# One transpose instruction for a whole cache tile, in a fused decode attention and gated MLP with gradients

## The chip, the cores and the metric

The kernel runs on one core of a Trainium2 chip. The metric is the time of the program on the device in microseconds; three runs of the kernel before gave a median of 469.5 us (469.31 to 469.81). One more execution was taken by the hardware profiler; its page and its trace are what is read here. Engines go by the profile's names: PE (TensorE), DVE (VectorE), ACT (ScalarE), POOL (GpSimd) and SP, which here only issues transfers.

## What is computed

The reference computes an output and all gradients (a vjp with a given `grad_out`) of one decode step:

```python
xn = layernorm(x)                                  # x: 2 x 1 x 576, bf16
q = (xn @ wq), 32 heads of 128                     # each pair of heads shares one of 16 cache heads
p = softmax(q . k_cache * 128**-0.5)               # caches: 2 x 16 x 4096 x 128
out = x + (p . v_cache) @ wo + ((xn @ w_gate) * (xn @ w_up)) @ w_down      # MLP width 4608
# returned: out and the gradients of x, k_cache, v_cache, wq, wo, w_gate, w_up, w_down
```

There is one query position, so the arithmetic is small beside the data: both caches and all weights are read once, and gradients of the same sizes are written. The gradient of each cache head is an outer product of 4096 values with the query or with the incoming gradient.

## The kernel before, in words

**Tiles.** A cache head of one batch row is 4096 x 128 bf16, 1 MB. It is loaded by one transfer into a tile of 128 partitions x 4096 elements (`kv_t`), 32 positions in each partition. Sixteen such buffers (`big`) are shared by cache tiles (at most 6), transposed tiles `X` (at most 10), store tiles `st` (at most 5) and MLP weights; they are handed out as they come free. A step `s` (16 in all) treats two cache heads of one batch row: two tiles of K and two of V, 64 cache tiles in all. Two steps make a group, which also has a slice of `wq` and of `wo`; the MLP goes in nine slices beside the groups.

**A cache tile's way.** `load_kv` (L1133) loads it from SP's queue. `turn` (L1208) takes an `X` buffer and transposes the tile into it on DVE. The transpose (`t32`, L464, recorded as L465) works on 32 x 32 blocks, and the bf16 data is seen as fp32 words, so that two neighbouring bf16 elements, a pair, move together: 4096 elements are 2048 pairs in each partition. `turn` does this in two halves of 1024 pairs, and sets the event `xE` after the second. Only then do the scores start: `score` (L1261, matmuls of L1267) reads columns from all over `X`, for K in `softmax` (L1317), for V in `dscore` (L1373). The untransposed tile is read once more by `contract` (L1424, matmuls of L1441), which sums over positions. When that and the transposes are done, `free_kv` (L1419) gives the cache buffer back, and the next load may be issued.

**The softmax chain.** It is a ping-pong of short instructions. DVE takes the maximum of each partition (`ex`, `mx`, L1330), PE turns it, DVE reduces it (`m`, L1340), ACT spreads it (`mr`, L1342), PE multiplies (L1344), DVE makes the bias (`negb`, L1346), ACT takes the exponential (L1349), PE sums (L1352), DVE inverts (`rz`, L1354), ACT scales, PE spreads, ACT or DVE copies (`sp`), and DVE transposes the result (`pp`). `dscore` is alike for the gradient of the scores: DVE multiplies and sums (`ds`, `cs`, L1385), PE sums over partitions (L1391), DVE makes `cr` (L1393) and `ds` (L1396), PE spreads it, ACT or DVE copies it (`sp`), DVE transposes it (`dd`). From `pp` and `dd` the outer products (L1289) make the gradients of the caches: `unit` (L698) has PE fill two PSUM banks, and ACT (L469) or DVE (L471) copy 1024 columns of them to a store tile; `put` (L691, transfer at L695) stores it. Smaller DVE copies serve a group's projections: `qd` (L992), `rep` (L1006), `oT` (L1461), `rT`.

**What sets the order.** The kernel does not leave the order to a scheduler of the compiler. Every piece of work is a Python generator that asks the planner `Order` (L105) for an engine and a time before it records its instructions: `yield DVE(1.25)` asks for 1.25 us of DVE, and the instructions that follow in the generator are recorded when the planner grants it. Requests have priorities (`pr`); buffers and events are planned as well. So each engine has a fixed order in which its instructions run, one behind the other, and what an engine waits for holds all that is behind it. `turn` asks twice for each tile, and between the two grants the planner may put other work on DVE.

Of the kernel before, what the change touches and what calls it, by code (L numbers as in the profile page):

```python
# [250 lines left out]
def DVE(cost):  # L251
    return ("op", "DVE", cost)
# [14 lines left out]
def ACQ(tag):  # L267
    return ("acq", tag)
# [6 lines left out]
def WAIT(*events):  # L275
    return ("wait", events)


def SET(event):
    return ("set", event)  # L280
# [6 lines left out]
def PRIO(prio):  # L287
    return ("prio", prio)
# [59 lines left out]
def pr(name, s):  # L348
    edge = {} if type(s) is not int else HEAD if s < 2 else TAIL if s > 13 else {}
    return STEP * s + PR[name] + edge.get(name, 0) + OFF.get(name, {}).get(int(s), 0)  # L350
# [3 lines left out]
def kernel(  # L354
# [106 lines left out]
    def pairs(ap):  # L461
        return ap.bitcast(FP32)

    def t32(out, in_):  # L464
        nc.vector.transpose(out, in_)  # L465
# [742 lines left out]
    def turn():  # L1208
        for s in range(NS):
            for t in range(2):  # L1210
                yield PRIO(pr(f"turn{t}", s))
                for l in range(G):
                    yield WAIT(kvL[s][t][l], *([] if s + t == 0 else [grp[s // Bq]["Ed" if t else "Eq"]]))
                    x = yield ACQ("X")
                    src = kv_t[kvS[s][t][l]]
                    for h in range(2):
                        yield DVE(1.25)
                        t32(pairs(X_t[x][:, 2048 * h:2048 * h + 2048]), pairs(src[:, 2048 * h:2048 * h + 2048]))
                    xS[s][t][l] = x
                    yield SET(xE[s][t][l])  # L1220

# [335 lines left out]
    for gen in (turn(), fronts(), build_W(0), build_W(1), build_BD(), attend(), dscores(), backs()):  # L1557
        od.spawn(gen, 0.0)
# [33 lines left out]
```

## Time and profile before

| | |
|---|---|
| median of three runs | 469.5 us |
| profiled execution, its own time | 469.68 us |
| its span, from the first to the last instruction | 467.9 us |
| DVE: busy, instructions | 373.8 us, 711 |
| transposes of a `big` tile from a `big` tile (L465, 1024 pairs) | 146, 176.3 us in all, 1224 ns each |
| evictions on DVE (L471) and on ACT (L469) | 81.3 us (75), 272.5 us (303) |
| moved by DMA | 185.97 MB, 397 GB/s on average |
| load of a K tile, a V tile, from issue to landing (median) | 14.5 us, 13.5 us |

Of the 146 transposes 128 are the halves of cache tiles; 18 serve the MLP weights (L938 and below) and are not touched. A line of a timeline or of a list of groups gives the start and the length in us (or busy us and the mean in ns), the engine, the line of the code, and what was written and read; the bracket at its end tells how long the engine had been idle before, and what released it. The chain that ended last is followed back from the last instruction, at each step to what released it. A slice of the page's rows is a fortieth of the span, 11.7 us.

### The profile page before, as it was taken

How to read it: one execution, taken by the hardware profiler on the slowest of the kernel's cores; microseconds unless marked ns; L12 is line 12 of the kernel's file. 1: busy time of each engine (PE TensorE's matmuls, PEld its weight loads, DVE VectorE, ACT ScalarE, POOL GpSimd, SP SyncE). 2: the span in 40 equal slices, each digit the busy share in tenths (PEclk: the TensorE clock that was granted, in tenths of full speed). 3: DMA queues.
4: the chain of work that ended last, by engine and by line, in shares of the span. 5: the costliest groups of instructions: out<-in, count | busy, mean ns of one | idle time of the engine just before them, and what ended most of it. 6: DMA issues, size and time to landing. Idle time of an engine off the chain costs nothing.

```text
span 467.9 us, 15712 instructions
## 1 busy us (share of the span) xinstructions
PE 378.5 (81%) x6750; PEld 216.3 (46%) x6750; DVE 373.8 (80%) x711; ACT 334.6 (72%) x512; POOL 143.6 (31%) x174
## 2 busy tenths in 40 slices
PE   1688779697987888797888887789988988988886
PEld 1445455465443444454555354455524433544443
DVE  8887888797589897769987779788878866877883
ACT  3268648788786787665867775678778968787874
POOL 0740044303316443470016341500643316033200
PEclk9966775987566666756775676755666665666865
DMA  8999999999999999999999999999999999999995
GB/s 300 417 407 423 409 423 396 415 411 330 418 423 406 410 424 410 421 416 421 404 398 416 414 415 405 378 345 366 419 415 424 420 414 426 422 351 393 420 367 207
DMA packets 40710, 185.97 MB, mean 397 GB/s; under 512 B 3640, under 2 KB 12352, under 8 KB 24256
## 3 DMA queue, kind: packets, MB, share of 16 engines
q1 hardware_dynamic: 40636, 184.96, 98.5%
q8 instruction: 53, 0.87, 0.7%
q14 instruction: 17, 0.14, 0.1%
q10 hardware_dynamic: 4, 0.00, 0.0%
HBM read 92.48 MB, written 92.48 MB: 395 GB/s over the span
## 4 chain that ended last, share of the span: by engine, by line
DMA 45%; PE 24%; DVE 13%; ACT 9%; SPq 4%; issue 4%; POOL 1%; DVEq 0%; ACTq 0%; POOLq 0%
DMA big<-in_A_v_cache_dram 22%; DMA out_dram<-big 15%; ACT big L469 7%; DVE big L465 7%; DMA ww<-in_B_w_down_dram 4%; PE ps_o L1289 4%; DMA big<-in_B_w_up_dram 4%; PE ps_m L1441 3%; PE ps_m L1267 3%; DVE big L471 3%; PE ps_o L726 3%; PE ps_o L763 2%; SPq L1191 2%; SPq L1197 1%; PE ps_m L677 1%
## 5 line engine op out<-in xcount | busy, mean ns | idle before, releaser
L469 ACT CAST big<-ps_o 128x1024 bf16<-128x1024 f32 (+2 forms) x303 | 272.5, 956 | 51.4 <-PE ps_o L1289 29.5
L465 DVE STREAM_TRANSPOSE big<-big 128x1024 f32<-128x1024 f32 x146 | 176.3, 1224 | 18.9 <-DMA big<-in_A_v_cache_dram 5.3
L1255 POOL TENSOR_TENSOR BD<-vr,mask 128x2048 bf16<-128x2048 bf16 x32 | 115.3, 3605 | 121.1 <-PE ps_o L1289 43.0
L471 DVE CAST big<-ps_o 128x1024 bf16<-128x1024 f32 (+1 forms) x75 | 81.3, 1087 | 15.3 <-PE ps_o L1289 5.7
L1267 PE MATMUL ps_m<-big,W 128*32 128x128 bf16 x2048 | 61.1, 284 | 3.0 <-issue 1.7
L1232 POOL COPY W<-rep 32x16 bf16<-32x16 bf16 x128 | 24.9, 194 | 116.5 <-DVE rep L1006 95.5
L1267 PEld LDWEIGHTS <-W 128*32 128x32 bf16 x2048 | 48.0, 127 | 22.0 <-issue 21.1
L1289 PE MATMUL ps_o<-BD,pp 32*128 32x512 bf16 x256 | 45.6, 492 | 13.1 <-ACT big L469 8.0
L1289 PE MATMUL ps_o<-BD,dd 32*128 32x512 bf16 x256 | 45.5, 525 | 9.2 <-ACT big L469 6.8
L465 DVE STREAM_TRANSPOSE big<-ww 128x1152 f32<-128x1152 f32 (+1 forms) x25 | 33.0, 1321 | 4.5 <-DMA out_dram<-big 2.4
L1441 PE MATMUL ps_m<-big,pp 128*32 128x512 bf16 x256 | 31.5, 576 | 3.4 <-DVE pp L465 3.1
L1441 PE MATMUL ps_m<-big,dd 128*32 128x512 bf16 x256 | 29.7, 556 | 1.2 <-DVE dd L465 0.9
L1289 PEld LDWEIGHTS <-pp 32*128 32x128 bf16 x256 | 10.2, 97 | 32.9 <-issue 24.5
L1289 PEld LDWEIGHTS <-dd 32*128 32x128 bf16 x256 | 10.2, 99 | 24.7 <-issue 17.1
L1038 POOL COPY qr<-qd 128x256 bf16<-128x256 bf16 x8 | 3.2, 397 | 54.0 <-DVE qd L471 43.2
L763 PEld LDWEIGHTS <-xnr 32*128 32x128 bf16 x368 | 13.0, 122 | 13.0 <-issue 12.2
L726 PE MATMUL ps_o<-dyr,R 32*32 32x288 bf16 x256 | 17.3, 388 | 1.6 <-ACT big L469 1.5
L726 PE MATMUL ps_o<-dyr,hb 32*32 32x288 bf16 x288 | 15.9, 334 | 2.4 <-ACT big L469 2.2
L763 PE MATMUL ps_o<-D,xnr 32*128 32x128 bf16 x256 | 14.6, 293 | 3.9 <-issue 2.2
L1451 ACT ACTIVATE osb<-ps_m 128x512 bf16<-128x512 f32 x15 | 8.9, 596 | 8.6 <-PE ps_m L1441 8.3
L887 PE MATMUL ps_m<-big,Wdy 128*128 128x128 bf16 x162 | 14.8, 262 | 0.0
L677 PE MATMUL ps_m<-big,wm 128*32 128x128 bf16 x416 | 13.3, 287 | 1.3 <-DVE qd L992 0.6
(205 smaller groups left out, 489.6 us busy)
## 6 DMA issues: line engine op xcount, KB each, us to landing
out_dram<-big SPq DMA_DIRECT2D x74, 1024.0 KB, 13.6
big<-in_A_k_cache_dram SPq DMA_DIRECT2D x32, 1024.0 KB, 14.5
big<-in_A_v_cache_dram SPq DMA_DIRECT2D x32, 1024.0 KB, 13.5
out_dram<-big SPq DMA_DIRECT2D x17, 576.0 KB, 10.7
ww<-in_B_w_down_dram SPq DMA_DIRECT2D x9, 576.0 KB, 12.6
ww<-in_A_wo_dram SPq DMA_DIRECT2D x8, 576.0 KB, 8.4
ww<-in_A_wq_dram SPq DMA_DIRECT2D x8, 512.0 KB, 11.6
big<-in_B_w_gate_dram SPq DMA_DIRECT2D x4, 1024.0 KB, 14.5
```

What stands on the lines that cost most here:

```text
L465: nc.vector.transpose(out, in_)
L469: nc.scalar.copy(out, in_)
L471: nc.vector.tensor_copy(out=out, in_=in_)
L677: nc.tensor.matmul(dp[32 * q:32 * q + 32, 0:P], lhsT=W, rhs=view(X, 0, P, xoff(q, s), [[FS, 4], [2, 32]]), start=(s == 0), stop=(s == S - 1))
L726: nc.tensor.matmul(o[32 * q:32 * q + 32, aa, 0:HD2], lhsT=view(t, 32 * q, 32, 2 * A + aa, [[4, 32]]), rhs=dyr[32 * q:32 * q + 32, k * HD2: ...
L763: nc.tensor.matmul(o[:, aa, j * P:(j + 1) * P], lhsT=xnr[32 * a:32 * a + 32, dc * P:(dc + 1) * P], rhs=rhs(a), start=True, stop=True)
L887: nc.tensor.matmul(dh, lhsT=Wdy[:, e, 2 * k:2 * k + P], rhs=view(X[:], 0, P, 64 * k + e, [[D, FC], [2, 32]]), start=(k == 0 and e == 0), s ...
L1232: nc.gpsimd.tensor_copy(view(W_t[t][w][:], 32 * a, 32, 6 + 8 * a, [[G * WW, 4], [WW, G], [1, 2]]), view(rep_t[grp[g]["qs"]][:], 32 * a, 32 ...
L1255: nc.gpsimd.tensor_tensor(BD_t[i][:], view(vr_t[v][:], 0, P, 0, [[0, 16], [1, Dh]]), view(mask16[:], 0, P, 0, [[1, 16], [0, Dh]]), ALU.mult)
L1267: nc.tensor.matmul(sc[32 * cq:32 * cq + 32, :], lhsT=view(W[:], 0, P, (be * G + l) * WW + 6 - 4 * c2 - 2 * l, [[1, 32]]), rhs=view(X[:], 0 ...
L1289: nc.tensor.matmul(o[:, k, :], lhsT=pr2[32 * c4:32 * c4 + 32, :], rhs=BD[32 * c4:32 * c4 + 32, 8 * l + 4 * h2:8 * l + 4 * h2 + 4, :], star ...
L1441: nc.tensor.matmul(ct[32 * j:32 * j + 32, :], lhsT=view(rT, 0, P, 4 * c + 2 * l, [[1, 32]]), rhs=kv_t[kvS[s][t][l]][:, Dh * c:Dh * (c + 4) ...
```

## The change

`turn` records one transpose for the whole tile, 2048 pairs, where it recorded two for 1024 pairs each. Both requests to the planner stay, and stand on both sides of the one instruction, so the planner sees the same work and plans the same order as before. The one instruction is recorded at the place of the first half; what the planner put between the halves now stands behind the whole transpose. `xE` is set after the second request, as before.

```diff
                     src = kv_t[kvS[s][t][l]]
-                    for h in range(2):
-                        yield DVE(1.25)
-                        t32(pairs(X_t[x][:, 2048 * h:2048 * h + 2048]), pairs(src[:, 2048 * h:2048 * h + 2048]))
+                    yield DVE(1.25)
+                    t32(pairs(X_t[x][:]), pairs(src[:]))
+                    yield DVE(1.25)
                     xS[s][t][l] = x
                     yield SET(xE[s][t][l])
```

The orders of PE, ACT, POOL and SP are the same in both kernels. DVE has 64 instructions fewer. In 15 of the 64 tiles the halves stood directly one behind the other; in the other 49 one to six instructions stood between them.

## The prediction

> **What bounds the kernel now.** I read the page first: busy shares, DMA, chain.
>
> ```profile
> PE 378.5 (81%) x6750; PEld 216.3 (46%) x6750; DVE 373.8 (80%) x711; ACT 334.6 (72%) x512; POOL 143.6 (31%) x174
> ...
> GB/s 300 417 407 423 409 423 396 415 411 330 418 423 406 410 424 410 421 416 421 404 398 416 414 415 405 378 345 366 419 415 424 420 414 426 422 351 393 420 367 207
> ...
> DMA 45%; PE 24%; DVE 13%; ACT 9%; SPq 4%; issue 4%; POOL 1%; DVEq 0%; ACTq 0%; POOLq 0%
> ```
>
> DMA carries the span: most of the 40 slices move over 400 GB/s, and the chain that ended last is 45% transfers. But slices 10, 26 to 28 and 36 (330, 345 to 378, 351 GB/s) show that transfers were sometimes issued too late, and 46% of the chain is PE, DVE and ACT. There a late VectorE instruction lengthens the run. VectorE has 467.9 - 373.8 = 94.1 us free, so its busy time alone is not the limit; the moment at which each of its instructions ends is.
>
> **The price of the instruction.** The groups of VectorE by form give durations for three lengths:
>
> ```profile
> L465 DVE STREAM_TRANSPOSE big<-ww 128x1152 f32<-128x1152 f32 x17 | 23.2, 1365 | 3.2 <-DMA out_dram<-big 1.1 <-issue 1.1 <-DMA ww<-in_B_w_down_dram 0.9
> ...
> L465 DVE STREAM_TRANSPOSE big<-ww 128x1024 f32<-128x1024 f32 x8 | 9.8, 1227 | 1.3 <-DMA out_dram<-big 1.3
> ...
> L465 DVE STREAM_TRANSPOSE Xt<-big 128x512 f32<-128x512 f32 x6 | 4.0, 672 | 0.0
> ```
>
> From 1024 to 1152 pairs costs 138 ns, 1.08 ns a pair; from 512 to 1024 costs 555, also 1.08. So 2048 pairs should take 1225 + 1024 x 1.08 = 2.33 us. What two halves take today stands in VectorE's timeline:
>
> ```profile
> 349.75 2.35 DVE L465 STREAM_TRANSPOSE big<-big 128x1024 f32<-128x1024 f32 x2
> 352.02 0.14 DVE L1461 CAST oT<-ps_m 128x4 bf16<-128x4 f32 x1
> ```
>
> Two halves end after 2.35 us, not 2.45, because an instruction starts some 0.08 to 0.1 us before the one ahead of it ends; the next one starts after 2.27. The whole tile would let its successor start after 2.33 - 0.08 = 2.25. I take a saving of 0.02 us a tile, 64 x 0.02 = 1.3 us of VectorE. Bounds: at best all that is fixed in an instruction goes, 2 x 672 - 1227 = 0.12 us, 7.5 us in all; at worst the long instruction is slower than its two halves by the spread of the row (1190 to 1248 ns), 0.06 us, 3.7 us lost. [...]
>
> **What moves.** The diff keeps both requests to the planner, so PE, ACT, POOL and SP keep their order; only VectorE's changes. Where the planner put nothing between the halves (15 tiles) nothing else happens. In the other 49 tiles something stood between them, and now waits for the whole tile: it starts up to 1.1 us later (2.25 us after the tile's start instead of 1.15). The second half had covered the wait for the answer to it. The timeline of all engines shows one such place:
>
> ```profile
> 181.03 1.25 DVE L465 STREAM_TRANSPOSE big<-big 128x1024 f32<-128x1024 f32 x1
> ...
> 182.19 0.24 DVE L1340 TENSOR_REDUCE m<-ps_m 1x4 f32<-1x128 f32 x1
> 182.36 1.22 DVE L465 STREAM_TRANSPOSE big<-big 128x1024 f32<-128x1024 f32 x1
> 182.46 0.30 ACT L1342 COPY mr<-m 1x128 f32<-1x128 f32 x1 [0.37 <-DVE m L1340]
> ...
> 182.67 1.00 ACT L469 CAST big<-ps_o 128x1024 bf16<-128x1024 f32 x1
> ...
> 182.81 0.38 PE L1344 MATMUL ps_m<-one,mr 1*128 1x1 f32 x2
> ...
> 183.52 0.11 DVE L1346 TENSOR_SCALAR negb<-ps_m 128x1 f32<-128x1 f32 x1
> ```
>
> The maximum `m` is ready at 182.43; ACT spreads it, PE multiplies until 183.19, and `negb` follows: a round trip of some 0.8 us, all under the second half. After the change `m` starts at 181.03 + 2.25 = 183.28 and ends at 183.5, and `negb` starts at about 184.5: 1.0 us late, with VectorE idle meanwhile. Queued behind it on VectorE is an eviction (L471); on ACT the 1.00 us eviction behind `mr` waits just as long, and PE waits for the PSUM that they free, SP for the stores: its queue already waits 80.0 us for evictions of VectorE and 78.2 for those of ACT ahead of stores (L695).
>
> I went through the 49 tiles in the timeline in this way; times are starts of the first half:
> - `m` between, `negb` next (36.61, 181.03, 331.80, 354.58): 1.0 + 1.0 + 1.0 + 0.9 = 3.9 us.
> - `negb` between, `rz` next (19.81): 0.95.
> - `ex` and `mx` (L1330) between, `m` next (210.07, 399.53, 422.01): 0.3 + 0.4 + 0.5 = 1.2.
> - `cr` and `ds` between, `sp` or `dd` next (29.28, 151.74, 173.59, 369.30, 392.09): 0.5 + 0.45 + 0.7 + 0.45 + 0.45 = 2.55. From `ds` to `sp` the timeline shows 0.46 us (260.83 to 261.29).
> - a small copy whose answer from PE comes next (9.18 `xs`, 128.75 `oT`, 131.27 `rT`, 324.86 `qd`): 1.0 + 0.5 + 0.95 + 0.9 = 3.35.
>
> In sum 11.95 us of new waits. Elsewhere the tile now covers a wait that stood in front of the instruction between: 1.31 us (tile of 277.67), 0.73 (221.55), 0.56 (104.50), 0.49 (287.80), 0.38 (240.40), 0.34 (344.55) and six of 0.12 to 0.32, together 5.2 us. VectorE's own line is thus 11.95 - 5.2 - 1.3 = 5.4 us longer, beside 94 us of slack.
>
> **What reaches the end.** The chain in order of time has pieces of VectorE at these places:
>
> ```profile
> 181.03 1.25 DVE big L465
> 182.27 0.16 DVE m L1340
> 182.43 1.15 DVE big L465
> 183.58 0.04 DVE negb L1346
> ```
>
> Of the new waits, those at 36.61 (1.0), 173.59 (0.7), 181.03 (1.0), 210.07 (0.3), 354.58 (0.9) and 399.53 (0.4) lie on it, and those at 128.75 and 131.27 touch it through ACT and PE with about 0.2 each: 4.7 us. The others fall into its transfers (22 to 36, 146 to 157, 321 to 335, 381 to 399, 403 to 432 us), where the DMA queue hides them: a 1 MB transfer lands 13.5 to 14.5 us after its issue, while 1 MB at 420 GB/s is 2.5 us, so it mostly waits behind others. The covered waits lie beside the chain. For pairs on the chain the shorter instruction gives back about 0.2. Of the 4.5 us left I take a quarter off, because lateness ahead of a transfer that has to queue anyway is partly absorbed: 3.5 us. The profiled execution took 469.68 us (467.9 of span and 1.8 around it), 0.18 over the median of 469.5. So 469.5 + 3.5 = **473.0 us**.
> [...]
>
> **Rivals.**
> - *Faster: the tile is complete sooner.* The scores (L1267) wait for the whole tile, so splitting never helped them. Where much stood between, the tile ends far earlier: the tile of 277.67 takes 7.24 us from its start to its end and would take 2.3, 4.9 us less; that of 245.67 3.0 us less, those of 240.40 and 359.77 2.2 each. Then scores start and cache buffers come free sooner, and loads are issued sooner. Against it: in front of a cache load (L1142) SP's queue waits 16.9 us for stores, 8.7 for earlier loads and 7.4 for the contraction (L1441), and no transpose is among the longest. Price: the 5.2 us of covered waits and half of the 1.3 to 7.5 us of saving, at the chain's share of compute (about half): 3 to 4.5 us, so 465 to 466.5. It decides if the order of loads, not the softmax, sets the end. Chance 0.28.
> - *Hidden:* the DMA queue absorbs both; 469.5 within 1 us. For it: 94 us of slack. Against it: the slices of 330 to 378 GB/s, where it ran dry. Chance 0.12.
> - *The delay spreads:* ACT and PE take their instructions in order, so every new wait also holds evictions behind it, and all 12 us arrive: 481.5. Chance 0.12.
> - *The instruction gives no saving* (0.06 us slower a tile): 3.7 us of VectorE, less than half of it on the chain, within the forecast's own range.
>
> **How the numbers follow.** The forecast (470.4 to 478) has 0.48. The range 465.5 to 480.5 leaves out about 0.1 on each side. The repeated runs differ by 0.5 us, so 0.2% (0.94 us) is about the smallest change that a measurement can tell. Faster 0.28, same 0.12, slower 0.12 + 0.48 = 0.60.
>
> **What would show it.** Right: 64 instructions of 2.3 us on L465; `negb`, `sp` and `rz` with more idle time in front of them on VectorE, some 5 us in all; ACT's waits for `m` and `negb` longer; more slices of the GB/s row under 400. Wrong: a duration far from 2.33 us, VectorE's idle time unchanged, or cache loads issued earlier with fewer thin slices.

## The result, and the profile after

The changed kernel took 474.64 us (median of 4 runs, 472.96 to 476.85), the kernel before 469.52 beside it: ratio 1.0112, 95% interval 1.0087 to 1.0137, so 4.1 to 6.4 us slower. The four runs lie in two pairs, 473.0 and 476.2 to 476.9; the profiled execution (476.23 us, span 474.4) is one of the upper; what parts the pairs was not found. All experiments below are ratios to the kernel before on the same chip.

The page after, with the engines' busy time and the DMA rate in 40 slices:

```profile
PE 379.1 (80%) x6750; PEld 217.6 (46%) x6750; DVE 370.7 (78%) x647; ACT 334.1 (70%) x512; POOL 143.3 (30%) x174
...
GB/s 306 413 408 374 380 406 380 415 399 358 307 394 420 406 425 406 424 416 409 416 413 412 420 424 402 389 349 358 415 425 421 419 413 424 390 334 395 421 388 204
```

DVE is busy 3.0 us less and the span is 6.5 us longer: its time without work rose from 94.1 to 103.7 us (sums of the unrounded trace). Slices 4, 5 and 7 (35 to 59 and 71 to 83 us), which moved 423, 409 and 396 GB/s before, moved 374, 380 and 380; slice 11 fell from 418 to 307. After slice 11 the two rows differ little, but for slices 12 (394 for 423) and 35 (390 for 422). The page's chain of after breaks off at 198 us, so its shares are not set beside those of before.

The groups of DVE by line show what waits (the columns after the bar: busy us, mean ns, then us of idle time in front of the group and what ended it). Before:

```profile
L465 DVE STREAM_TRANSPOSE big<-big 128x1024 f32<-128x1024 f32 x146 | 176.3, 1224 | 18.9 <-DMA big<-in_A_v_cache_dram 5.3 <-DMA big<-in_A_k_cache_dram 5.1 <-DMA out_dram<-big 3.9
...
L1354 DVE RECIPROCAL rz<-ps_m 128x1 f32<-128x1 f32 x16 | 2.5, 155 | 3.2 <-PE ps_m L1352 3.1
...
L1393 DVE TENSOR_TENSOR cr<-ps_m,rz 128x1 f32<-128x1 f32 x16 | 2.1, 131 | 1.4 <-PE ps_m L1391 1.4
...
L1346 DVE TENSOR_SCALAR negb<-ps_m 128x1 f32<-128x1 f32 x16 | 2.1, 130 | 2.7 <-PE ps_m L1344 1.6 <-PE ps_o L1289 1.1
```

After:

```profile
L465 DVE STREAM_TRANSPOSE big<-big 128x2048 f32<-128x2048 f32 (+1 forms) x82 | 168.2, 2059 | 5.9 <-DMA big<-in_A_v_cache_dram 2.9 <-DMA out_dram<-big 1.2 <-PE ps_m L1267 1.1
...
L1354 DVE RECIPROCAL rz<-ps_m 128x1 f32<-128x1 f32 x16 | 2.5, 157 | 5.9 <-PE ps_m L1352 5.7
...
L1393 DVE TENSOR_TENSOR cr<-ps_m,rz 128x1 f32<-128x1 f32 x16 | 2.1, 133 | 2.9 <-PE ps_m L1391 2.9
...
L1346 DVE TENSOR_SCALAR negb<-ps_m 128x1 f32<-128x1 f32 x16 | 2.3, 143 | 6.3 <-PE ps_m L1344 4.5 <-PE ps_o L1289 1.8
```

The small instructions of the softmax wait more, mostly for PE (`negb` +3.6, `rz` +2.7, `cr` +1.5 us; `ex`, not shown, +3.3), while the transposes of the first row wait 13 us less, most of it for transfers (V loads 5.3 before, 2.9 after; stores 3.9 and 1.2). The 64 whole tiles alone (first line), and the place that the prediction worked out, in DVE's timeline after:

```profile
L465 DVE STREAM_TRANSPOSE big<-big 128x2048 f32<-128x2048 f32 x64 | 146.7, 2296 | 4.7 <-DMA big<-in_A_v_cache_dram 2.9 <-PE ps_m L1267 1.1 <-DMA big<-in_A_k_cache_dram 0.6
...
185.96 2.31 DVE L465 STREAM_TRANSPOSE big<-big 128x2048 f32<-128x2048 f32 x1
188.19 0.24 DVE L1340 TENSOR_REDUCE m<-ps_m 1x4 f32<-1x128 f32 x1
189.23 0.16 DVE L1346 TENSOR_SCALAR negb<-ps_m 128x1 f32<-128x1 f32 x1 [0.80 <-PE ps_m L1344]
```

From the tile's start to `negb` are 3.27 us; before they were 183.52 - 181.03 = 2.49. The wait uncovered is 0.80 us, the round trip that had been counted, and `negb` is 0.78 us later than it would be.

Where the lateness of the whole kernel arises is seen by setting the same DVE instruction of the two traces side by side: 0.8 us late at 12 us (`gg`, L643), 3.1 at 32 (`dd`), 5.2 at 79 (`pp`), between 2.4 and 9.0 from there on, and 5.2 at 460. So as much as is left at DVE's end was there at 79 us. The other 1.3 of the 6.5 us lie behind DVE's last instruction, where the last small store is waited for: 4.6 us here and 3.3 before. In the traces of the other kernels below this stretch is 2.4 to 4.5 us, and does not follow the number of merged tiles. The first of it, before and then after:

```profile
19.81 1.22 DVE L465 STREAM_TRANSPOSE big<-big 128x1024 f32<-128x1024 f32 x1
20.96 0.11 DVE L1346 TENSOR_SCALAR negb<-ps_m 128x1 f32<-128x1 f32 x1
21.01 1.21 DVE L465 STREAM_TRANSPOSE big<-big 128x1024 f32<-128x1024 f32 x1
22.16 0.12 DVE L1354 RECIPROCAL rz<-ps_m 128x1 f32<-128x1 f32 x1
22.21 1.20 DVE L465 STREAM_TRANSPOSE big<-big 128x1024 f32<-128x1024 f32 x1
23.63 0.45 DVE L465 STREAM_TRANSPOSE pp<-sp 128x256 bf16<-128x256 bf16 x1 [0.22 <-ACT sp L469]
```

```profile
20.77 2.29 DVE L465 STREAM_TRANSPOSE big<-big 128x2048 f32<-128x2048 f32 x1
23.00 0.11 DVE L1346 TENSOR_SCALAR negb<-ps_m 128x1 f32<-128x1 f32 x1
24.31 0.17 DVE L1354 RECIPROCAL rz<-ps_m 128x1 f32<-128x1 f32 x1 [1.20 <-PE ps_m L1352]
24.40 2.29 DVE L465 STREAM_TRANSPOSE big<-big 128x2048 f32<-128x2048 f32 x1
26.61 0.40 DVE L465 STREAM_TRANSPOSE pp<-sp 128x256 bf16<-128x256 bf16 x1
```

`pp` of the first step starts 26.61 instead of 23.63, 3.0 us late: 1.0 was brought along, 1.1 come from the first tile here (`negb` behind the whole of it), and 0.8 from the next (`pp` behind the whole of that; this is tile 3, which the prediction did not count). The first store waits for outer products with this `pp`. SP's queue in the two traces, at its first store:

```profile
30.41 5.05 SPq L695 DMA_DIRECT2D out_dram<-big  x2
35.56 1.58 SPq L1142 DMA_DIRECT2D big<-in_A_k_cache_dram  x2
```

```profile
33.01 5.98 SPq L695 DMA_DIRECT2D out_dram<-big  x2
39.09 2.28 SPq L1142 DMA_DIRECT2D big<-in_A_k_cache_dram  x2
```

The first store goes out 2.6 us later, and the cache load behind it 3.5 us later.

### The profile page after: what moved, and what is told of

Same layout as the page of the kernel before. It is cut to its first block, busy times and chain, and to the rows that moved or that the text cites. A ratio compares the mean times of both kernels' runs of the same rounds, so it can differ in the third digit from the quotient of the medians.

```text
span 474.4 us, 15648 instructions
## 1 busy us (share of the span) xinstructions
PE 379.1 (80%) x6750; PEld 217.6 (46%) x6750; DVE 370.7 (78%) x647; ACT 334.1 (70%) x512; POOL 143.3 (30%) x174
## 4 chain that ended last, share of the span: by engine, by line
PE 22%; DVE 14%; DMA 11%; ACT 6%; issue 4%; SPq 0%; DVEq 0%; ACTq 0%
DVE big L465 10%; DMA big<-in_A_v_cache_dram 8%; ACT big L469 5%; PE ps_m L1441 4%; PE ps_o L1289 4%; PE ps_m L1267 3%; DMA out_dram<-big 2%; PE ps_o L726 2%; DVE big L471 2%; PE ps_o L763 1%; PE ps_m L677 1%; PE ps_m L887 1%; PE ps_m L1344 1%; PE ps_m L1352 0%; PE ps_m L1022 0%
## 5 line engine op out<-in xcount | busy, mean ns | idle before, releaser
L465 DVE STREAM_TRANSPOSE big<-big 128x2048 f32<-128x2048 f32 (+1 forms) x82 | 168.2, 2059 | 5.9 <-DMA big<-in_A_v_cache_dram 2.9
L1441 PE MATMUL ps_m<-big,dd 128*32 128x512 bf16 x256 | 28.6, 538 | 0.8 <-DVE dd L465 0.6
L726 PE MATMUL ps_o<-dyr,R 32*32 32x288 bf16 x256 | 19.2, 430 | 1.3 <-ACT big L469 1.3
L887 PEld LDWEIGHTS <-Wdy 128*128 128x128 bf16 x162 | 13.5, 121 | 3.8 <-issue 3.6
L469 ACT CAST vr<-ps_m 128x128 bf16<-128x128 f32 x24 | 6.6, 275 | 11.1 <-PE ps_m L1247 11.1
```

The costliest lines, as they stand in the source:

```text
L469: nc.scalar.copy(out, in_)
L726: nc.tensor.matmul(o[32 * q:32 * q + 32, aa, 0:HD2], lhsT=view(t, 32 * q, 32, 2 * A + aa, [[4, 32]]), rhs=dyr[32 * q:32 * q + 32, k * HD2: ...
L887: nc.tensor.matmul(dh, lhsT=Wdy[:, e, 2 * k:2 * k + P], rhs=view(X[:], 0, P, 64 * k + e, [[D, FC], [2, 32]]), start=(k == 0 and e == 0), s ...
L1441: nc.tensor.matmul(ct[32 * j:32 * j + 32, :], lhsT=view(rT, 0, P, 4 * c + 2 * l, [[1, 32]]), rhs=kv_t[kvS[s][t][l]][:, Dh * c:Dh * (c + 4) ...
```

## The experiments

Two theories came from the two traces. **A**: the loss is made before the stores get going, and the DMA queue takes up the rest. **B**, the prediction's own: new waits all along the chain add up. Most kernels below choose, for each tile (number 4s + 2t + l, in order of time), whether it is turned whole or in halves. The edit is the same, and only the condition differs:

```diff
                     for h in range(2):
                         yield DVE(1.25)
-                        t32(pairs(X_t[x][:, 2048 * h:2048 * h + 2048]), pairs(src[:, 2048 * h:2048 * h + 2048]))
+                        if whole and h == 0:
+                            t32(pairs(X_t[x][:]), pairs(src[:]))
+                        if not whole:
+                            t32(pairs(X_t[x][:, 2048 * h:2048 * h + 2048]), pairs(src[:, 2048 * h:2048 * h + 2048]))
```

### The early steps alone

`whole = s < 3`, 12 tiles.

> One transpose for the whole tile in steps 0 to 2 only (the first 12 of 64 tiles, all before 83 us); halves in the rest. Theory A, from the two traces: the loss is made before the stores get going, since VectorE's instructions are already 3.1 us late at 32 us and 5.2 us late at 79 us, and 5.2 us late at the end: 473.0 to 476.0 us. Theory B, as the prediction had it: new waits at many places of the chain add up over the whole run, and only one of them (1.0 us, tile of 36.61) lies in these steps: 469.5 to 471.0.

Measured: 472.3 us, ratio 1.0044 (1.0024 to 1.0064): 1.1 to 3.0 us slower, between the ranges of the two theories.

### All the others

`whole = s >= 3`, 52 tiles.

> Halves in steps 0 to 2, one transpose for the whole tile in steps 3 to 15 (52 tiles). Theory A: the DMA queue takes up what is late after the first steps: 469.0 to 471.0. Theory B: 3.7 of the 4.7 us on the chain lie here: 472.0 to 474.0.

Measured: 472.05 us, ratio 1.0037 (1.0022 to 1.0051), 1.0 to 2.4 us; by its median at the lower edge of B's range, above A's. Neither A nor B holds alone: 12 tiles lose about as much as the other 52. Together the two make 3.8 us of the 5.1 of the full change; the intervals allow 2.1 to 5.4, so whether anything is missing is open.

### Is it the instruction or the order?

Two halves, both at the place of the first:

```diff
-                    for h in range(2):
-                        yield DVE(1.25)
+                    yield DVE(1.25)
+                    for h in range(2):
                         t32(pairs(X_t[x][:, 2048 * h:2048 * h + 2048]), pairs(src[:, 2048 * h:2048 * h + 2048]))
+                    yield DVE(1.25)
```

> Two halves as before, but both recorded at the place of the first: the order of the changed kernel with the instructions of the one before. If the order makes the loss, as both A and B say: 473.5 to 477.5, 0 to 2 us over the changed kernel, since two halves take 0.06 us longer than the whole (2.35 against 2.29). Rival C, that the long instruction itself is to blame (it holds VectorE for 2.29 us without a break): 469.0 to 470.5.

Measured: 475.82 us, ratio 1.0123 (1.0097 to 1.0149): with the instructions of before, as slow as the change. Its DVE timeline has the same hole in front of `rz`:

```profile
20.30 2.35 DVE L465 STREAM_TRANSPOSE big<-big 128x1024 f32<-128x1024 f32 x2
22.59 0.11 DVE L1347 TENSOR_SCALAR negb<-ps_m 128x1 f32<-128x1 f32 x1
23.90 0.17 DVE L1355 RECIPROCAL rz<-ps_m 128x1 f32<-128x1 f32 x1 [1.21 <-PE ps_m L1353]
```

So the order is to blame; C falls.

### The whole tile at the place of the second half

```diff
-                    for h in range(2):
-                        yield DVE(1.25)
-                        t32(pairs(X_t[x][:, 2048 * h:2048 * h + 2048]), pairs(src[:, 2048 * h:2048 * h + 2048]))
+                    yield DVE(1.25)
+                    yield DVE(1.25)
+                    t32(pairs(X_t[x][:]), pairs(src[:]))
```

> One transpose for the whole tile, recorded at the place of the second half: what stood between the halves now goes ahead of the tile. The waits for that are then no longer covered by the first half (0.8 to 1.0 us in front of negb, 0.2 to 1.3 elsewhere), but what follows the tile is covered twice over. Theory A and B: of the same kind as the changed kernel, 471.0 to 476.0, with new idle time in front of the instructions that stood between. Rival D, that only the delay of the softmax chain costs (this order starts it earlier): 467.5 to 470.0.

Measured: 474.65 us, ratio 1.0095 (1.0073 to 1.0116). D falls. The groups of DVE in this kernel:

```profile
L1354 DVE RECIPROCAL rz<-ps_m 128x1 f32<-128x1 f32 x16 | 2.5, 156 | 7.8 <-PE ps_m L1352 7.8
...
L1393 DVE TENSOR_TENSOR cr<-ps_m,rz 128x1 f32<-128x1 f32 x16 | 2.4, 152 | 6.8 <-PE ps_m L1391 6.8
```

`rz` and `cr` wait 4.6 and 5.4 us longer than before. Either way round, one of two round trips loses its cover.

### The 17 tiles with a counted wait, and the other 47

`whole = 4 * s + 2 * t + l in (0, 2, 5, 6, 16, 17, 21, 25, 26, 30, 45, 47, 50, 53, 56, 58, 62)`, and then `not in`.

> One transpose for the whole tile only in the 17 tiles for which the prediction counted a new wait on VectorE (11.95 us together); halves in the other 47. Theory E, that these waits make the loss: 472.5 to 476.0. Rival F, that any shift of VectorE's order costs something, wherever it lies (32 other tiles have something between their halves): 470.5 to 472.0.

Measured: 472.03 us, ratio 1.0059 (1.0044 to 1.0074), 2.1 to 3.5 us, just below E's range: 27% of the tiles make about half of the loss.

> The complement: halves in those 17 tiles, one transpose in the other 47. Theory E: without the new waits only what is saved is left (64 instructions less 17, 0.06 us each, and 5.2 us of covered waits): 467.0 to 470.0, that is no slower than before. Rival F: 472.0 to 474.0.

Measured: 470.44 us, ratio 1.002 (1.0005 to 1.0034), 0.2 to 1.6 us, above E's range and below F's. The 47 others, 32 of them with something between, lose a third as much as the 17. But they lose; the saved instructions and the covered waits did not bring a gain, as E had it. The sum of the two is 3.7 us, and the intervals allow 2.3 to 5.1.

### The saving alone, and the saving with the covered waits

`whole` in the 15 tiles 1, 4, 7, 18, 20, 22, 33, 36, 40, 44, 49, 52, 55, 57, 61.

> One transpose only in the 15 tiles whose halves stood one behind the other, so that the order of VectorE's instructions does not change at all; halves elsewhere. What is left is the saving of 0.04 to 0.06 us for each, 0.6 to 0.9 us of VectorE: 469.0 to 470.2 by every theory that blames the order. If the long instruction itself costs: 470.5 to 472.0.

Measured: 470.4 us, ratio 1.0015 (1.0000 to 1.0031). With 10, 11, 15, 24, 29, 31, 34, 35, 39, 41, 48, 51 added:

> One transpose in those 15 tiles and in the 12 where the prediction counted a wait that the whole tile covers (5.2 us together); halves elsewhere. Theory E: the gains without the losses, 466.5 to 469.5. Rival F: 470.5 to 472.0.

Measured: 470.4 us, ratio 1.0021 (1.0003 to 1.0039), above E's range and just below F's. The covered waits are worth nothing that can be measured. For the 15 pairs alone the interval reaches from no difference to 1.5 us; whether merging costs something even where no order changes stays open, and a gain of their 0.6 us of DVE time is not there.

### Four tiles around the first store

`whole` in the tiles 0, 2, 5, 6.

> One transpose only in four tiles, those that start at 9.18, 19.81, 29.28 and 36.61 us, ahead of and around the first stores; halves in the other 60. Theory G, that the new waits there (1.0, 0.95, 0.5 and 1.0 us) put off the first stores and that the DMA queue runs dry for as long at 36 to 60 us: all that steps 0 to 2 lost, 471.3 to 473.0. Rival H, that the other eight tiles of these steps lose it: 469.5 to 470.8.

Measured: 471.54 us, ratio 1.0038 (1.0018 to 1.0059): all that the 12 tiles of the early steps lost (1.0044), by four of them; H falls. Three of the tiles start before the first store, the fourth after it. The stretches from 36 to 52 us, last column GB/s, in the kernel before and in this one:

```profile
36.00:44.00 8.00, 6.37 (x89) 4.19 (x89) 6.56 (x11) 6.46 (x12) 0.00 (x0) 0.69 1.01 424
44.00:52.00 8.00, 6.97 (x162) 3.90 (x155) 6.41 (x14) 6.84 (x11) 0.00 (x0) 0.88 1.03 409
```

```profile
36.00:44.00 8.00, 5.94 (x111) 3.09 (x101) 6.44 (x9) 5.78 (x10) 0.00 (x0) 0.89 1.00 377
44.00:52.00 8.00, 6.32 (x166) 3.96 (x166) 6.20 (x16) 7.79 (x13) 0.00 (x0) 1.00 1.00 365
```

(424 + 409 - 377 - 365) x 8 us = 0.73 MB that were not moved, 1.7 us at 424 GB/s, behind a first store that came 2.2 us late (32.62). This dip comes with the four tiles. In the traces of all six kernels that turn each of the four at one place these stretches moved 354 to 399 and 365 to 382 GB/s, with the first store at 32.1 to 33.6 us; in those of the six others that keep them in halves, 422 to 427 and 406 to 411 GB/s, with the first store at 30.7 to 31.4.

That the dip is what the kernel loses (1.8 us by the ratio, 0.8 to 2.8 by its interval) its trace does not show. DVE is 2.1 us late up to `D` (89.32 us before) and 0.1 us late at `dd` behind it. The wait in front of `dd`, and the one of ACT ahead of it, before and then in this kernel:

```profile
93.05 0.45 DVE L465 STREAM_TRANSPOSE dd<-sp 128x256 bf16<-128x256 bf16 x1 [3.34 <-ACT sp L469]
...
89.89 2.84 ACT L469 CAST big<-ps_o 128x1024 bf16<-128x1024 f32 x3 [2.44 <-DMA out_dram<-big]
```

```profile
93.17 0.45 DVE L465 STREAM_TRANSPOSE dd<-sp 128x256 bf16<-128x256 bf16 x1 [1.34 <-ACT sp L469]
...
90.02 2.84 ACT L469 CAST big<-ps_o 128x1024 bf16<-128x1024 f32 x3 [0.39 <-DMA out_dram<-big]
```

ACT had waited 2.44 us for a store to land; that store lands at about the same time here, and the lateness is gone. At DVE's last instruction this execution is 0.5 us late, and most of its longer span (469.6 for 467.9) lies behind that. Of the first half of G a late first store (32.62 us for 30.41) and a lower DMA rate are shown. A dry DMA queue is not: the DMA engines' busy share, the column before the rate, was 1.00 in both stretches, for 1.01 and 1.03 before. How the 1.8 us of the ten runs reach the end is not shown either.

### The other thirteen, and all but the four

`whole` in the 13 later of the 17 tiles.

> One transpose only in the other 13 tiles with a new wait (8.5 us together, from 128 us on); halves elsewhere. Theory G: the DMA queue takes up most of it, 469.8 to 471.0. Theory B of the prediction (3.5 of its 4.7 us on the chain lie here): 472.5 to 474.0.

Measured: 470.3 us, ratio 1.002 (0.9999 to 1.0040), 0 to 1.9 us, within G's range. B falls, by which 3.7 of the 4.7 us lie here (the expectation put it at 3.5). All tiles but 0, 2, 5, 6:

> One transpose in all tiles but those four. Theory G: about 2.2 us less than the changed kernel, 471.0 to 473.0. Rival H: hardly less than the changed kernel, 473.5 to 475.5.

Measured: 472.38 us, ratio 1.0059 (1.0035 to 1.0084), within G's range and below H's. Against the full change (1.0112) the four tiles in halves give back about half of the loss.

### Planned with the true length

```diff
-                    for h in range(2):
-                        yield DVE(1.25)
-                        t32(pairs(X_t[x][:, 2048 * h:2048 * h + 2048]), pairs(src[:, 2048 * h:2048 * h + 2048]))
+                    yield DVE(2.32)
+                    t32(pairs(X_t[x][:]), pairs(src[:]))
```

> The whole tile by one instruction, asked for by one request of 2.32 us, so that the planner knows its length and plans the order of all engines anew (PE, ACT, POOL, SP and VectorE all differ from the kernel before). Theory J, that the loss comes only from an order that was planned for halves: 468.5 to 471.5. Rival K, that a 2.3 us instruction on an engine that runs in order has no good place in a chain of short ones, whoever plans it: 472.0 to 480.0.

Measured: 479.97 us, ratio 1.0232 (1.0201 to 1.0263). J falls. Its page and its groups of DVE:

```profile
GB/s 295 413 409 285 387 423 407 415 347 307 331 391 420 412 421 410 422 419 419 418 409 414 402 241 410 397 386 361 412 420 423 421 409 427 423 378 377 410 391 235
```

```profile
L465 DVE STREAM_TRANSPOSE big<-big 128x2048 f32<-128x2048 f32 (+1 forms) x82 | 168.2, 2059 | 19.2 <-DMA big<-in_A_v_cache_dram 13.7 <-DMA out_dram<-big 4.9 <-DMA big<-in_A_k_cache_dram 0.2
```

Slices 4 and 24 fall to 285 and 241 GB/s, and transposes wait 13.7 us for V tiles. Since every engine's order differs here, this says only that this plan is worse, not that none could be good; the priorities are still those of the kernel with halves. No version that was run beats the kernel before.

## Why the prediction was right, and where its steps were off

- *Price of the instruction.* Forecast 2.33 us with 2.25 to the next start; measured 2.30 (mean 2296 ns) and 2.23 (185.96 to 188.19). Against 2.27 for two halves that is 0.04 us a tile and 2.6 us in all, not 1.3; DVE was busy 3.0 us less. The time of the run, 5.1 us longer, shows no gain from it.
- *What moves.* Right. Instructions between the halves start about 1.07 us late (seen in the steps of the two traces against each other), round trips lose their cover, and two_first shows that this order alone makes the loss.
- *New waits, 11.95 us in 17 tiles.* Right in kind: `negb` waits 0.80 us where 1.0 was counted, `rz` 1.20 where 0.95 was. The 17 tiles made 2.8 us of the 5.1. But other tiles count as well (0.9 us). In the three splits the parts add up to 3.8, 3.7 and 4.6 us; the intervals leave open whether that is less than the whole, and what the tiles do to each other was not traced further.
- *What reaches the end: this step failed in its places.* It said that the waits off the chain "fall into its transfers", "where the DMA queue hides them", and that 4.7 us lie on the chain from 36.61 us on. The runs show it otherwise. The 13 later tiles, which had 3.7 of the 4.7 us, cost 0.9 (0 to 1.9). Three of the four early tiles had been put at nothing, and these four, with 1.0 us on the chain, cost 1.8 (0.8 to 2.8); the first twelve cost 2.1 (1.1 to 3.0). Of the tiles put at nothing, those at 9.18, 19.81 and 369.30 lie in none of the stretches that the prediction names. Early on nothing has been stored yet (the first store leaves at 30.41 us before); in the changed kernel that store is 2.6 us late and the load behind it in SP's queue 3.5 us, and from 36 to 52 us the DMA moves 354 and 376 GB/s for 424 and 409. Which path then carries the loss to the end stays open. The traces are single executions: DVE's last instruction is 3.7 to 5.7 us late in the four kernels of this planned order that turn all twelve early tiles whole, and between 1.4 us early and 0.5 us late in the eight others, the four tiles alone among these. The chain followed back from the end showed a V load issued at 22.11 and landing at 36.59, and could not show what a late first store does.
- *The size,* 3.5 against 5.1 us, came near by luck: the late tiles were counted too high, the early ones too low, and the 47 others not at all. (Three quarters of 4.5 are 3.4 us, not 3.5.)
- *Rivals.* Faster by earlier tiles: falls with covered_whole (1.0021), where the tile of 277.67 is complete 5.0 us sooner. Hidden: falls as a whole; the 13 late tiles come near it (0 to 1.9 us). All 12 us arrive: falls. No saving: falls, there is a saving, and it brings nothing.

## What to carry to other kernels

A long instruction cut in two on an engine that runs in order need not be mere overhead: here its halves were the cover for two round trips of a chain of short instructions, and merging them left one of the two bare (0.80 us in front of `negb` at 189.23, 1.20 in front of `rz` at 24.31). Ask where in the run a delay falls: here four tiles around the first store cost 1.8 us (0.8 to 2.8), and thirteen later ones with more than twice the counted waits 0.9 (0 to 1.9). And ask what a dip in the DMA row leaves at the end before calling it the loss: behind the dip of 1.7 us in early4_whole DVE was on time again some 40 us later. Busy time saved on an engine with time to spare need not shorten the run: here DVE, without work for 94.1 us of the span before, was busy 3.0 us less and the run took 5.1 us longer.

## What was not expected of the hardware

A transposed pair cost 1.05 ns beyond the first 1024 (2296 - 1224 = 1072 ns for 1024 pairs), a little less than the 1.08 ns between 512, 1024 and 1152. The granted TensorE clock averaged 0.687 in the profiled execution after and 0.680 before, so a lower clock is not what made the loss.
